# Attention and gated MLP for one token: A_w_down's first chunk in A_wo's column groups, K heads 0 and 1 in two transfers

## The chip, the cores and the metric

The kernel runs on one core of a Trainium2 chip. The core has five engines with instruction streams of their own (TensorE or PE for matmuls, VectorE or DVE, ScalarE or ACT, GpSimd or POOL, SyncE or SP, which here issues the DMAs), an on-chip memory of 128 partitions (SBUF), and a matmul accumulator of 128 partitions by eight banks of 512 float32 (PSUM). The metric is device time in microseconds (us) of one execution, as the median over runs; smaller is better.

## The reference, cut to what matters

One token x of 512 values is normalized, and two branches start from the result. Branch A is attention: 32 query heads over the last 4096 positions of a cache with 8 key and value heads of 128, then the output weight wo. Branch B is a gated MLP of width 1792; with one token in the batch its routing always picks that token, and only the sigmoid of the routing score is left of it.

```python
xn = layernorm(x)
# A: x @ wq -> 32 heads of 128; W = 4096 positions; 4 query heads share one K/V head
scores = einsum("bhqd,bhkd->bhqk", q, k) * 128 ** -0.5
o = softmax(scores) @ v
a = o.reshape(1, 1, 4096) @ wo                      # 4096 x 512
# B: one token, so the top-1 choice is that token
y = (silu(xn @ w_gate) * (xn @ w_up)) @ w_down      # 512 x 1792, 1792 x 512
b = xn + y * sigmoid(xn @ w_r)
return x + a + b
```

All inputs are bfloat16. 30.7 MB are read from device memory: 4.2 MB of wq, 8.4 MB each of K and V, 3.7 MB of w_gate and w_up together, 4.2 MB of wo, 1.8 MB of w_down.

## The kernel before, in words

The program is written out by hand for each engine. `Eng.mark` makes an instruction count up its engine's semaphore, and `Eng.need` makes an engine wait until a semaphore has reached a mark. Each DMA has a semaphore of its own, which sixteen DMA engines count up. `hoist` at the end moves the first issues ahead of the program's start; it changes no order within an engine.

**Transfers.** SP issues all large ones, in this order: wq in two halves (L110, L209), K in four transfers of two heads (L220, `pair`), V in four (L325), then, once the query projection has read wq, w_gate and w_up into wq's place (L327, L328), and, once six K heads have been copied out of `k_sb`, wo in two halves and w_down in four chunks of 7, 4, 2 and 1 rows per partition (L407 to L413) into K's place. They form one queue. A row here is what one partition holds of w_down for one of 14 steps; a chunk of seven rows is 128 pieces of 7 KB.

`pair` brings positions of two heads at once: 64 partitions belong to each head, and a partition's 64 positions of 128 values are 16 KB in one piece. With `steps([0, 2, 4, 6, 8])` each transfer carries two of the kernel's "heads", which are halves of those 64 positions.

**Queries.** TensorE waits for a half of wq and multiplies it with xn in 16 matmuls (L300), four at a time in four column groups of the array (`tile_position`). ACT copies the result (L306), TensorE transposes it in two halves (L320), and DVE spreads each half into `qpad` (`q_out`, L308 to L313). The first half's `q_out` runs right there (L323), the second's stands behind DVE's first two K copies (L354 to L356).

**K stage** (L354 to L405). For each of eight heads DVE copies the head from `k_sb` to `kin` in two halves (`C`, L344), TensorE transposes it in four blocks (`T`, L380), DVE and ACT evacuate the blocks (`E`, L349 and L352), and TensorE multiplies them with the queries (`Sm`, L389) into the two score banks 4 and 5. Then come the softmax (L422 to L445), the V stage with a loop over eight heads (L449 to L504), the gate and up matmuls (L524), and the products behind them on DVE (L535 to L540), which leave w_down's left operand in `hTr`.

**End.** TensorE multiplies wo's 32 rows in four column groups into bank 5 (`grouped`, `a_ps`, L546): row j goes to partition 32 * (j % 4), so that four matmuls of 512 columns run at once, and the first four start the accumulation. DVE adds the four partial rows to the residual (`rf`, zero but for partition 0) and writes `part` (L565). w_down's 14 rows go by halves into banks 0 and 1 (`by_halves`, L551): two column groups, each with 256 columns. Behind the first chunk TensorE adds `part` up over its four partitions with a vector of ones at those places (`sel4`, float32, by halves into the same two banks, L573). Behind the last chunk DVE and ACT each copy one half of the result, and SP sends it out (L578 to L581).

**Fillers.** Matmuls of zeros into bank 7, which nobody reads, stand at many places (`warm`, `fill`; L191): among them two behind the normalization (L268), one before the second half of wq (L295), a loop of five times two before the K stage (L357), four behind L529 (`fill(F4)`), a loop of eight times two between wo's halves (L560), and four behind wo (L564).

Of the kernel before, what the change touches and what calls it, by code (L numbers as in the profile page):

```python
# [9 lines left out]
ALU = mybir.AluOpType  # L10
# [28 lines left out]
def kernel(  # L39
# [15 lines left out]
    P = 128  # L55
    D = A_x.shape[2]
    KT = D // P
    HKV = A_k_cache.shape[1]
# [7 lines left out]
    FB = F // P  # L66
    RJ = (HQ * DH) // P
# [35 lines left out]
    def early(eng, name, out_, in_):  # L103
# [13 lines left out]
    k_sb = sb("k_sb", [P, HKV, 4, 1024], BF16)  # L117
# [7 lines left out]
    qpad = sb("qpad", [P, HKV, 2, 32], BF16)  # L125
# [4 lines left out]
    hTr = sb("hTr", [P, FB, 32], BF16)  # L130
# [5 lines left out]
    zst = sb("zst", [P, P], BF16)  # L136
    zmov = sb("zmov", [P, 512], BF16)
# [18 lines left out]
    oT2 = sb("oT2", [P, RJ], BF16)  # L156
# [7 lines left out]
    ps = nc.alloc_psum_tensor("ps", [P, 8, 512], F32)  # L164
# [3 lines left out]
    qT_ps = ps[:, 6, 0:256].bitcast(BF16).rearrange("p (h c) -> p h c", c=P)  # L168
    pT_ps = ps[:, 0:2, :].bitcast(BF16)
    pv_ps = ps[:, 2, :]  # L170
    a_ps = ps[:, 5, :]
    HD = D // 2
    g_ps = [ps[32 * c:32 * c + 1, c, 0:HD] for c in range(2)]
    rf = kT[:, 0, :].bitcast(F32)
    part = kT[:, 1, :].bitcast(F32)
# [5 lines left out]
    wd_sb = k_flat[:, 0:FB * D]  # L181
    wo_sb = k_flat[:, FB * D:(FB + RJ) * D]

    S = lambda n: nc.alloc_semaphore(n)
    PE, ACT, DVE, POOL, SP = (Eng(nc, nc.tensor, "pe"), Eng(nc, nc.scalar, "act"), Eng(nc, nc.vector, "dve"),
                              Eng(nc, nc.gpsimd, "pool"), Eng(nc, nc.sync, "sp"))
    te, ac, ve, gp, sy = nc.tensor, nc.scalar, nc.vector, nc.gpsimd, nc.sync

    def warm(n):
        for _ in range(n):  # L190
            te.matmul(ps[:, 7, :], lhsT=zst[:], rhs=zmov[:], start=True, stop=True)  # L191

    def fill(n):
        warm(2 * n)

    def ends(ins):
        ends_at[ins.ins.engine] = ins.ins.name
# [14 lines left out]
    def pair(name, tile_, cache, i0, i1):  # L212
        g, n = i0 // 2, (i1 - i0) * NT
        src = cache[0, 2 * g:2 * g + 2, Sk - W:, :].rearrange("h (q t) d -> q h t d", t=TP)
        dst = bass.AP(tile_, i0 * NT * DH, [[HKV * NT * DH, P], [1, n * DH]])
        t0 = (i0 % 2) * NT
        return [dma(sy, f"{name}{i0}", dst, src[:, :, t0:t0 + n, :].rearrange("q h t d -> q h (t d)"))] * (i1 - i0)

    steps = lambda cuts: zip(cuts[:-1], cuts[1:])
    t_k = sum([pair("k", k_sb, A_k_cache, a, b) for a, b in steps([0, 2, 4, 6, 8])], [])  # L220

    c0 = POOL.mark(gp.memset(ident_bf[:], 0.0))
    POOL.need(c0)
# [4 lines left out]
    t_qpad0 = POOL.mark(gp.memset(qpad[:], 0.0))  # L228
# [11 lines left out]
    a = DVE.mark(ve.bn_stats(out=stats[:], in_=xrow[:]))  # L240
# [6 lines left out]
    a = DVE.mark(ve.reciprocal(out=sml[:, 1:2], in_=sml[:, 0:1]))  # L247
# [5 lines left out]
    for kt in range(KT):  # L253
        ins = te.matmul(ps[:, 6, 256 + kt:257 + kt], lhsT=xn_row[:].rearrange("a (p k) -> a k p", k=KT)[:, kt, :],  # L254
                        rhs=ident_bf[0:1, 0:1], start=True, stop=True)
# [9 lines left out]
    t_identf = DVE.mark(ve.tensor_copy(out=ident_f[:], in_=ident_bf[:]))  # L265
    DVE.need(t_rth)
    t_gf = DVE.mark(ve.tensor_scalar(out=sml[:, 4:5], in0=sml[:, 3:4], scalar1=0.25, scalar2=0.25, op0=ALU.mult, op1=ALU.add))
    warm(2)  # L268
    PE.need(t_gf, t_ones)
    t_gfp = PE.mark(te.matmul(ps[:, 6, 264:265], lhsT=ones_f[0:1, :], rhs=sml[:, 4:5], start=True, stop=True))  # L270
    with nc.allow_low_precision(reason="0/1 values are exact in bf16"):
# [4 lines left out]
                                     in_=ident_bf[:].rearrange("p (q h) -> p h q", h=2)))  # L276
# [13 lines left out]
    t_qpad = []  # L290
    for kh in range(2):
        if kh == 1:
            for ch in range(2):
                te.matmul(sc[:, ch, :], lhsT=zst[:], rhs=zmov[:], start=True, stop=False, skip_group_check=True)
            warm(1)  # L295
        PE.need(t_wq[kh], t_ps0)
        for hf in range(2):
            for kt in range(kh * KH, (kh + 1) * KH):
                for c in range(4):
                    ins = te.matmul(ps[32 * c:32 * c + 1, hf, :], lhsT=xnT[:, kt:kt + 1],  # L300
                                    rhs=wq_sb[:, kt, (4 * hf + c) * 512:(4 * hf + c + 1) * 512],
                                    start=(kt == 0), stop=(kt == KT - 1), tile_position=(0, 32 * c))
            if kh == 1:
                t_qp = PE.mark(ins)
                ACT.need(t_qp)
                t_qe.append(ACT.mark(ac.copy(out=q4[:, hf, :], in_=ps[:, hf, :])))  # L306

    def q_out(hf, t_qt):  # L308
        DVE.need(t_qt, t_qpad0)
        for u in range(2):  # L310
            dst = bass.AP(qpad, 2 * hf * 132 + 80 * u, [[HKV * 64, P], [132, 2], [32, 2], [1, 4]])
            t_q = DVE.mark(ve.tensor_copy(out=dst, in_=qT_ps.rearrange("p h (g e r) -> p g e h r", e=2, r=32)[:, :, :, :, 0]))
        t_qpad.append(t_q)  # L313

    for hf in range(2):
        PE.need(t_qe[hf], t_gfb)
        if hf == 1:
            PE.need(t_qpad[0])
        for hl in range(4):
            ins = te.transpose(qT_ps[:, hl, :], q4[:, hf, hl * DH:(hl + 1) * DH], ident_bf[:])  # L320
        t_qt = PE.mark(ins)
        if hf == 0:
            q_out(hf, t_qt)  # L323

    t_v = sum([pair("v", v_sb, A_v_cache, a, b) for a, b in steps([0, 2, 4, 6, 8])], [])  # L325
    SP.need(t_qp)
# [26 lines left out]

    for h in range(2):  # L354
        C(0, h)
    q_out(1, t_qt)  # L356
    with te.Fori(0, 5):  # L357
        warm(2)
    for g in range(HKV):
        pool_q(g)  # L360
        last = (g == HKV - 1)
# [35 lines left out]
    with te.Fori(1, 9) as i:  # L397
# [20 lines left out]
    a = POOL.mark(gp.memset(rf, 0.0))  # L418
    POOL.need(a)
    t_rf = POOL.mark(gp.tensor_copy(out=rf[0:1, :], in_=resid[:]))  # L420
# [13 lines left out]
                              start=True, stop=True))  # L434
# [49 lines left out]
    with te.Fori(1, 9) as i:  # L484
        g = i - 1
# [52 lines left out]
                                           in1=ps[:, 3, 0:FC].rearrange("p (i b) -> p b i", b=FB), op0=ALU.mult, op1=ALU.mult))  # L538
    DVE.need(t_h)
    t_hT = DVE.mark(ve.transpose(out=hTr[:].rearrange("p b i -> p (b i)"), in_=h4[:].rearrange("p b i -> p (b i)")))  # L540
    fill(F4)
    PE.need(t_oT2)

    def grouped(j, lhsT, w):
        c = j % 4
        return te.matmul(a_ps[32 * c:32 * c + 1, :], lhsT=lhsT, rhs=w[:, j * D:(j + 1) * D], start=(j < 4), stop=False,  # L546
                         tile_position=(0, 32 * c), skip_group_check=True)

    def by_halves(lhsT, row, start=False, stop=False):
        for c in range(2):  # L550
            ins = te.matmul(g_ps[c], lhsT=lhsT, rhs=row[:, c * HD:(c + 1) * HD], start=start, stop=stop,  # L551
                            tile_position=(0, 32 * c), skip_group_check=True)
        return ins

    for k, (j0, j1) in enumerate(wo_chunks):
        PE.need(t_wo[k])
        for j in range(j0, j1):
            ins = grouped(j, oT2[:, j:j + 1], wo_sb)
        if k == 0:
            with te.Fori(0, 8):  # L560
                fill(1)
    t_g4 = PE.mark(ins)
    DVE.need(t_g4, t_rf)
    fill(2)  # L564
    t_part = DVE.mark(ve.tensor_tensor(out=part, in0=a_ps, in1=rf, op=ALU.add))  # L565
    PE.need(t_hT)
    for k, (j0, j1) in enumerate(wd_chunks):
        PE.need(t_wd[k])
        for j in range(j0, j1):
            ins = by_halves(hTr[:, j, 0:1], wd_sb[:, j * D:(j + 1) * D], start=(j == 0), stop=(j == FB - 1))  # L570
        if k == 0:
            PE.need(t_part, t_sel4)
            by_halves(sel4[:], part)  # L573
    t_a = PE.mark(ins)
# [38 lines left out]
```

## Time and profile before

| what | value |
|---|---|
| median of 4 runs | 78.96 us (78.89 to 79.05) |
| the profiled execution | 78.89 us |
| its span, first to last instruction | 77.3 us |
| read from device memory | 30.67 MB, mean 397 GB/s over the span |
| busy share: TensorE, its weight loads | 75%, 38% |
| busy share: DVE, ACT, POOL | 57%, 39%, 14% |
| the chain that ended last, by engine | DMA 70%, PE 14%, ACT 6%, DVE 3% |

The busy shares are means over stages with different limits. The chain of waits goes back from the last instruction to what released it, step by step, and so names what the end hangs on. In the rows of the time line the first number is the start in us from the span's start, the second the length, and the bracket names how long the engine idled before and what ended that wait. A row can hold several matmuls of one line (x14), which overlap each other. The granted clock is the one that the throttle granted to TensorE; it is 1.0 throughout. The trace also has one record for each DMA packet (start, length, bytes, queue); sixteen engines work in parallel, each through its own share of every transfer, with a 4-byte packet, the semaphore, behind each share.

### The profile page before, as it was taken

What the parts mean: (1) busy time and instruction counts of PE and PEld (TensorE: products, weight loads), DVE (VectorE), ACT (ScalarE), POOL (GpSimd) and SP (SyncE); (2) the same over time, 40 slices, a digit from 0 to 9 for tenths busy, and PEclk for the clock granted to TensorE, in tenths of its full rate; (3) what the DMA queues carried; (4) which work ended last, traced back from release to release, by engine and by line L of the source; (5) the groups of instructions that cost most, each with busy time, mean ns of one, the idle gap of its engine ahead of it and who ended that gap; (6) DMA issues with size and microseconds to landing.
All of it is one profiled execution on the core that took longest, in us unless ns stands there. A gap on an engine that the chain in (4) does not pass through costs nothing.

```text
span 77.3 us, 1662 instructions
## 1 busy us (share of the span) xinstructions
PE 57.8 (75%) x645; PEld 29.7 (38%) x652; DVE 43.8 (57%) x96; ACT 30.4 (39%) x41; POOL 10.6 (14%) x22
## 2 busy tenths in 40 slices
PE   0015985767989997997995766788887795798891
PEld 0010411426766775685682225222222251343240
DVE  2765900119866956966963762988989248400302
ACT  2771003102895895896775043333343420000001
POOL 3960000000230220220217600000000000000000
DMA  6999999999999999999999999999999999999910
GB/s 136 398 416 407 415 475 432 432 415 407 432 475 441 415 407 415 449 432 441 419 398 424 449 441 432 424 405 423 445 408 465 423 415 407 441 404 405 377 43 1
DMA packets 2601, 30.72 MB, mean 397 GB/s; under 512 B 291, under 2 KB 422, under 8 KB 806
## 3 DMA queue, kind: packets, MB, share of 16 engines
q1 hardware_dynamic: 2594, 30.67, 94.3%
q8 instruction: 2, 0.03, 0.2%
q14 instruction: 1, 0.01, 0.0%
q10 hardware_dynamic: 4, 0.00, 0.0%
HBM read 30.67 MB, written 0.00 MB: 397 GB/s over the span
## 4 chain that ended last, share of the span: by engine, by line
DMA 70%; PE 14%; ACT 6%; DVE 3%; issue 2%; SPq 1%
DMA k_sb<-in_B_w_down_dram 51%; DMA k_sb<-in_A_k_cache_dram 20%; PE ps L380 8%; ACT kT L352 6%; PE ps L551 3%; PE ps L389 3%; DVE kin L344 2%; SPq L202 1%; DVE kT L349 1%; DVE kT L578 1%; SPq L84 0%; SPq L101 0%
## 5 line engine op out<-in xcount | busy, mean ns | idle before, releaser
L352 ACT COPY kT<-ps 128x1024 bf16<-128x1024 bf16 x19 | 18.6, 1016 | 9.5 <-PE ps L380 9.4
L380 PE MATMUL ps<-perm_bf,kin 128*128 128x128 bf16 x256 | 17.1, 220 | 1.4 <-DVE kin L344 1.0
L380 PEld LDWEIGHTS ps<-perm_bf,kin 128*128 128x128 bf16 x256 | 14.3, 98 | 5.8 <-issue 4.3
L344 DVE COPY kin<-k_sb 128x2048 bf16<-128x2048 bf16 x16 | 10.9, 686 | 5.2 <-DMA k_sb<-in_A_k_cache_dram 3.7
L191 PE MATMUL ps<-zmov,zst 128*128 128x512 bf16 x38 | 10.9, 394 | 1.7 <-PEq L84 1.2
L349 DVE COPY kT<-ps 128x1024 bf16<-128x1024 bf16 x13 | 9.0, 691 | 2.9 <-PE ps L380 2.4
L475 ACT CAST pvS<-ps 128x512 bf16<-128x512 f32 x8 | 4.7, 586 | 10.0 <-PE ps L481 10.0
L337 POOL COPY qAB<-qpad 128x64 bf16<-128x64 bf16 x8 | 4.0, 500 | 31.2 <-PE ps L389 31.2
L389 PE MATMUL ps<-kT,qAB 128*32 128x512 bf16 x68 | 6.8, 389 | 1.9 <-ACT kT L352 1.9
L191 PEld LDWEIGHTS ps<-zmov,zst 128*128 128x128 bf16 x45 | 3.9, 99 | 6.2 <-issue 3.3
L455 DVE COPY vin<-v_sb 128x2048 bf16<-128x2048 bf16 x8 | 5.5, 685 | 1.1 <-PE ps L490 1.0
L461 DVE COPY vin<-v_sb 128x2048 bf16<-128x2048 bf16 x8 | 5.5, 683 | 0.0
L490 PE MATMUL ps<-vin,pTcur 128*32 128x512 bf16 x32 | 3.2, 386 | 2.6 <-ACT pvS L475 2.2
L579 ACT CAST kT<-ps 1x256 bf16<-1x256 f32 x1 | 0.4, 363 | 11.9 <-PE ps L551 11.9
L502 PE MATMUL ps<-zmov,zst 128*128 128x512 bf16 x16 | 4.7, 376 | 0.0
L254 PE MATMUL ps<-ident_bf,xn_row 1*128 1x1 bf16 x4 | 0.3, 166 | 5.1 <-POOL qAB L231 5.1
L565 DVE TENSOR_TENSOR kT<-ps,kT 128x512 f32<-128x512 f32 x1 | 0.7, 691 | 5.5 <-PE ps L546 5.5
L300 PE MATMUL ps<-wq_sb,xnT 128*1 128x512 bf16 x32 | 2.9, 499 | 0.8 <-DMA wq_sb<-in_A_wq_dram 0.8
L496 PE MATMUL ps<-vin,pTcur 128*32 128x512 bf16 x32 | 3.2, 387 | 0.3 <-DVE vin L461 0.2
L490 PEld LDWEIGHTS ps<-vin,pTcur 128*32 128x32 bf16 x32 | 1.1, 92 | 6.0 <-DVE vin L455 5.5
L389 PEld LDWEIGHTS ps<-kT,qAB 128*32 128x32 bf16 x68 | 1.9, 92 | 3.9 <-DVE kT L349 1.1
L306 ACT CAST q<-ps 128x512 bf16<-128x512 f32 x2 | 1.1, 588 | 5.3 <-PE ps L300 5.3
(92 smaller groups left out, 52.3 us busy)
## 6 DMA issues: line engine op xcount, KB each, us to landing
k_sb<-in_A_k_cache_dram SPq DMA_DIRECT2D x4, 2048.0 KB, 21.8
v_sb<-in_A_v_cache_dram SPq DMA_DIRECT2D x4, 2048.0 KB, 38.4
wq_sb<-in_A_wq_dram SPq DMA_DIRECT2D x2, 2048.0 KB, 9.1
k_sb<-in_A_wo_dram SPq DMA_DIRECT2D x2, 2048.0 KB, 35.1
wq_sb<-in_B_w_gate_dram SPq DMA_DIRECT2D x1, 1792.0 KB, 43.6
wq_sb<-in_B_w_up_dram SPq DMA_DIRECT2D x1, 1792.0 KB, 47.5
k_sb<-in_B_w_down_dram SPq DMA_DIRECT2D x1, 896.0 KB, 39.1
k_sb<-in_B_w_down_dram SPq DMA_DIRECT2D x1, 512.0 KB, 39.9
```

Source lines behind the costliest of these rows:

```text
L191: te.matmul(ps[:, 7, :], lhsT=zst[:], rhs=zmov[:], start=True, stop=True)
L337: gp.tensor_copy(out=qAB[:], in_=qpad[:, g]).then_inc(s_q, 1)
L344: ve.tensor_copy(out=kin[:, 2 * h:2 * h + 2, :], in_=k_sb[:, g, 2 * h:2 * h + 2, :]).then_inc(s_c[h], 1)
L349: ve.tensor_copy(out=kT[:, b, :], in_=tp[:, b, :]).then_inc(s_ev[b], 1)
L352: ac.copy(out=kT[:, b, :], in_=tp[:, b, :]).then_inc(s_ev[b], 1)
L380: ins = te.transpose(tp[:, b, k * P:(k + 1) * P], kin[:, b, k * P:(k + 1) * P], perm_bf[:])
L389: ins = te.matmul(sc[32 * cq:32 * cq + 32, e, :], lhsT=qAB[:, e, :], rhs=kT[:, b, :].rearrange("d (k h q) -> d h k q", h=2, q=PH)[:, e], s ...
L455: ve.tensor_copy(out=vin[:, 0].rearrange("p (q k) d -> p q (k d)", q=4), in_=v_in[:, :, 0:4 * DH]).then_inc(s_va, 1)
L461: ve.tensor_copy(out=vin[:, 1].rearrange("p (q k) d -> p q (k d)", q=4), in_=v_in[:, :, 4 * DH:]).then_inc(s_vb, 1)
L475: ac.copy(out=pvS[:].rearrange("p t d -> p (t d)"), in_=pv_ps).then_inc(s_pvs, 1)
L490: ins = te.matmul(pv_ps[32 * tl:32 * tl + 32, :], lhsT=pTcur[:, tl].rearrange("p q e r -> p (q e r)"), rhs=vin[:, 0].rearrange("p (q t) d ...
L502: te.matmul(ps[:, 7, :], lhsT=zst[:], rhs=zmov[:], start=True, stop=True)
```

## The change

Four things differ.

- K's first two heads come in two transfers (256 pieces of 8 KB in place of 128 of 16 KB), each with its own semaphore.
- The second half's `q_out` moves up to the first, ahead of DVE's first K copies, and the fillers at L268, L295 and L357 are gone.
- w_down's first chunk of seven rows goes through `grouped`, into bank 5 on top of wo's partial rows. For that bank 5 and the halves of banks 0 and 1 are zeroed by three matmuls of zeros ahead of `fill(F4)`, and no later matmul starts an accumulation there.
- DVE's addition of the residual waits for that chunk, and the matmuls with `sel4` stand behind the second chunk instead of the first. Behind wo there are two fillers in place of four.

```diff
-    def warm(n):
-        for _ in range(n):
+    def fill(n):
+        for _ in range(2 * n):
             te.matmul(ps[:, 7, :], lhsT=zst[:], rhs=zmov[:], start=True, stop=True)
-
-    def fill(n):
-        warm(2 * n)
...
-    t_k = sum([pair("k", k_sb, A_k_cache, a, b) for a, b in steps([0, 2, 4, 6, 8])], [])
+    t_k = sum([pair("k", k_sb, A_k_cache, a, b) for a, b in steps([0, 1, 2, 4, 6, 8])], [])
...
-    warm(2)
     PE.need(t_gf, t_ones)
...
                 te.matmul(sc[:, ch, :], lhsT=zst[:], rhs=zmov[:], start=True, stop=False, skip_group_check=True)
-            warm(1)
...
-    def q_out(hf, t_qt):
-        DVE.need(t_qt, t_qpad0)
-        for u in range(2):
-            dst = bass.AP(qpad, 2 * hf * 132 + 80 * u, [[HKV * 64, P], [132, 2], [32, 2], [1, 4]])
-            t_q = DVE.mark(ve.tensor_copy(out=dst, in_=qT_ps.rearrange("p h (g e r) -> p g e h r", e=2, r=32)[:, :, :, :, 0]))
-        t_qpad.append(t_q)
...
         t_qt = PE.mark(ins)
-        if hf == 0:
-            q_out(hf, t_qt)
+        DVE.need(t_qt, t_qpad0)
+        for u in range(2):
+            dst = bass.AP(qpad, 2 * hf * 132 + 80 * u, [[HKV * 64, P], [132, 2], [32, 2], [1, 4]])
+            t_q = DVE.mark(ve.tensor_copy(out=dst, in_=qT_ps.rearrange("p h (g e r) -> p g e h r", e=2, r=32)[:, :, :, :, 0]))
+        t_qpad.append(t_q)
...
     for h in range(2):
         C(0, h)
-    q_out(1, t_qt)
-    with te.Fori(0, 5):
-        warm(2)
...
+    te.matmul(a_ps, lhsT=zst[:], rhs=zmov[:], start=True, stop=False, skip_group_check=True)
+    for c in range(2):
+        te.matmul(ps[:, c, 0:HD], lhsT=zst[:], rhs=zmov[:, 0:HD], start=True, stop=False, skip_group_check=True)
     fill(F4)
     PE.need(t_oT2)
 
-    def grouped(j, lhsT, w):
+    def grouped(j, lhsT, w, row):
         c = j % 4
-        return te.matmul(a_ps[32 * c:32 * c + 1, :], lhsT=lhsT, rhs=w[:, j * D:(j + 1) * D], start=(j < 4), stop=False,
+        return te.matmul(a_ps[32 * c:32 * c + 1, :], lhsT=lhsT, rhs=w[:, row * D:(row + 1) * D], start=False, stop=False,
                          tile_position=(0, 32 * c), skip_group_check=True)
 
-    def by_halves(lhsT, row, start=False, stop=False):
+    def by_halves(lhsT, row, stop=False):
         for c in range(2):
-            ins = te.matmul(g_ps[c], lhsT=lhsT, rhs=row[:, c * HD:(c + 1) * HD], start=start, stop=stop,
+            ins = te.matmul(g_ps[c], lhsT=lhsT, rhs=row[:, c * HD:(c + 1) * HD], start=False, stop=stop,
                             tile_position=(0, 32 * c), skip_group_check=True)
         return ins
 
     for k, (j0, j1) in enumerate(wo_chunks):
         PE.need(t_wo[k])
         for j in range(j0, j1):
-            ins = grouped(j, oT2[:, j:j + 1], wo_sb)
+            ins = grouped(j, oT2[:, j:j + 1], wo_sb, j)
         if k == 0:
             with te.Fori(0, 8):
                 fill(1)
-    t_g4 = PE.mark(ins)
-    DVE.need(t_g4, t_rf)
-    fill(2)
-    t_part = DVE.mark(ve.tensor_tensor(out=part, in0=a_ps, in1=rf, op=ALU.add))
+    fill(1)
     PE.need(t_hT)
     for k, (j0, j1) in enumerate(wd_chunks):
         PE.need(t_wd[k])
         for j in range(j0, j1):
-            ins = by_halves(hTr[:, j, 0:1], wd_sb[:, j * D:(j + 1) * D], start=(j == 0), stop=(j == FB - 1))
+            if k == 0:
+                ins = grouped(j + RJ, hTr[:, j, 0:1], wd_sb, j)
+            else:
+                ins = by_halves(hTr[:, j, 0:1], wd_sb[:, j * D:(j + 1) * D], stop=(j == FB - 1))
         if k == 0:
+            t_g4 = PE.mark(ins)
+            DVE.need(t_g4, t_rf)
+            t_part = DVE.mark(ve.tensor_tensor(out=part, in0=a_ps, in1=rf, op=ALU.add))
+        if k == 1:
             PE.need(t_part, t_sel4)
             by_halves(sel4[:], part)
```

## The prediction, made before the changed kernel ran

> **What bounds the kernel now.** I read the chain of waits first, then the time line of the last six microseconds, then the table of windows for the DMA at the end, then the trace's DMA packets one by one.
>
> The end of the chain of waits, in order of time (start, length, what):
>
> ```profile
> 34.02 39.12 DMA k_sb<-in_B_w_down_dram
> 73.14 0.14 issue
> 73.27 1.80 PE ps L551 x26
> 75.07 0.00 issue
> 75.08 0.62 PE ps L551 x6
> 75.70 0.03 issue
> 75.72 0.41 DVE kT L578
> ```
>
> The time line of the end (start, length, engine, line):
>
> ```profile
> 70.98 1.03 PE L546 MATMUL ps<-k_sb,oT 128*1 128x512 bf16 x16 [0.21 <-DMA k_sb<-in_A_wo_dram]
> 71.95 1.04 PE L191 MATMUL ps<-zmov,zst 128*128 128x512 bf16 x4
> 72.07 0.69 DVE L565 TENSOR_TENSOR kT<-ps,kT 128x512 f32<-128x512 f32 x1 [5.51 <-PE ps L546]
> 73.27 0.93 PE L551 MATMUL ps<-k_sb,hTr 128*1 128x256 bf16 x14 [0.29 <-DMA k_sb<-in_B_w_down_dram]
> 74.03 0.60 PE L551 MATMUL ps<-kT,sel 128*1 128x256 f32 x4
> 74.44 0.34 PEld L551 LDWEIGHTS ps<-k_sb,hTr 128*1 128x1 bf16 x8 [0.31 <-DMA k_sb<-in_B_w_down_dram]
> 74.47 1.21 PE L551 MATMUL ps<-k_sb,hTr 128*1 128x256 bf16 x14
> 75.07 0.09 PEld L551 LDWEIGHTS ps<-k_sb,hTr 128*1 128x1 bf16 x4 [0.30 <-DMA k_sb<-in_B_w_down_dram]
> 75.40 0.08 PEld L551 LDWEIGHTS ps<-k_sb,hTr 128*1 128x1 bf16 x2 [0.24 <-DMA k_sb<-in_B_w_down_dram]
> ```
>
> The windows (length, five engines, clock, DMA share, GB/s), and the instruction queues' rows of the page:
>
> ```profile
> 72.50:73.00 0.50, 0.49 (x3) 0.00 (x0) 0.26 (x1) 0.00 (x0) 0.00 (x0) 1.00 1.02 391
> 73.50:74.00 0.50, 0.50 (x14) 0.42 (x10) 0.00 (x0) 0.00 (x0) 0.00 (x0) 1.00 0.17 61
> 74.00:74.50 0.50, 0.50 (x10) 0.17 (x8) 0.00 (x0) 0.00 (x0) 0.00 (x0) 1.00 0.14 53
> ...
> q8 instruction: 2, 0.03, 0.2%
> q14 instruction: 1, 0.01, 0.0%
> ```
>
> The kernel is a DMA stream that is full from 1.0 us on. The four pieces of A_w_down reach TensorE at 73.17, 74.44, 75.07 and 75.40, and TensorE's weight loads wait for a DMA before the last three (0.31, 0.30, 0.24 us); only in front of the second were matmuls still running, the selecting ones, to 74.47. The last piece sets the end: 75.40, then 0.3 us of matmul, 0.41 of copy, 1.2 of the output's DMA: span 77.3, and 1.55 around it make the profiled run's 78.89. The median of the four runs, 78.96, is 0.07 above. So only two things count: when the DMA stream ends, and what TensorE does between 73.17 and 75.70.
>
> The windows show that the stream ends raggedly: after 73.5 the rate is 53 to 61 GB/s, two of sixteen engines. In the packets, fourteen engines write their last semaphore by 73.7, one at 74.52, one at 74.92. The last one stood still for 1.02 us at 29.79, while a 16 KB packet of the instruction queue q8 ran (29.78 to 30.82); the other lost its time at 37.89, beside the 8 KB packet of q14.
>
> **The change, part by part.**
>
> *K heads 0 and 1 in two transfers.* 128 pieces of 16 KB become 256 of 8 KB; one more issue on SP (0.59 to 0.66 us by the four K issues), which moves the V issues (4.29 to 8.37 us) back by that. V lands from 37 us on and SP then idles until 13.2 us: nothing. The stream itself gets slower. In the packets one engine takes 4.865 us for eight pieces of 16 KB with their semaphore (first engine done at 6.58, 11.45, 16.32, 21.18), 4.29 for eight of 14 KB (50.49 to 54.78), 2.17 for eight of 7 KB (68.87 to 71.04). A line through 7 and 16 KB gives 0.3085 us for 8 KB; sixteen of them take 4.94 instead of 4.865: +0.07. Halving 14 KB pieces into 7 KB gives 2 x 2.17 - 4.29 = +0.05. The floor is 0; a gain is excluded, since no row has smaller pieces running faster. I take +0.07, the nearest rows; it shifts all that comes after, the last piece too.
>
> The Trainium skill, "DMA: Bandwidth & Descriptors", Specifications, says that a transfer runs at line rate from 512 B up. By it this part would cost 0 and the sum would be 0.07 less; the rows (26.4 GB/s per engine in 7 KB pieces, 26.9 in 16 KB) do not agree with it to that precision.
>
> Head 0 can start after 1 MB. DVE's first copy began at 17.06 after waiting 2.89; half of the 4.87 us earlier is 14.6. q_out(1), two copies of 0.13, now stands before it on DVE and waits for the second transposes (end 14.69), so the copy starts at 15.0. Queued behind q_out on DVE are these copies, and TensorE's first K transposes wait for them. DVE has one more wait, for head 1's own semaphore, before C(1,0), with the evacuation of head 0's third block queued behind it; head 1 lands at about 17.06 and DVE would be there at 17.1: nothing. Head 2 still comes with its transfer: DVE waited 0.86 for it at 21.95. The two microseconds are lost there, and the K stage goes on as before.
>
> *Fillers removed.* Two at 6.58, one at 10.88, ten at 14.75 to 16.9, two of four at 71.95, against three zeroing matmuls more behind L529. The latter cost 0.216 + 2 x 0.109 = 0.43 us after 64.99; A_wo's first half reaches TensorE at 66.07, which covers them and leaves 0.65. The two behind A_wo ended at 72.99, before 73.17: TensorE waits for the DMA instead, 0. The early ones can let the clock fall: the first 16 query matmuls took 1.88 us (8.24), the second 16, after fillers, 1.03 (12.19), at a granted clock of 1.00 in both. If the second also run slow: +0.85, transposes twice 0.4 more, K's first copy at 16.3 instead of 15.0, still before 17.06. Slow K transposes (16 in 1.07 now, 1.95 at that ratio) over heads 0 and 1 could at worst put the compute chain 1 to 2 us late; behind it lie 0.65 before A_wo, 0.2 before its second half, 0.7 before 73.17, together 1.5. I take 0.
>
> The skill's "TensorE: Matmul & The Clock Gate", Part 1, says that an idle window of about 3.4 us halves the clock. That speaks against removing the ten; no run here shows how long an idle stretch the clock bears. With head 0 here at 14.6 TensorE would idle about 1 us in front of the K stage, so by the rule the sum has 0 for these ten as well.
>
> *The tail, where the path is.* In place of 14 half-row matmuls, A_w_down's first seven rows run in four column groups: two rounds. A_wo's 16 give (1.03 - 0.378)/3 = 0.217 a round. From 73.27: 0.217 + 0.378, end 73.87; DVE starts 0.06 later (72.01 to 72.07 now), 0.69: the sum is ready at 74.62. It was ready at 72.76. TensorE meanwhile waits for the second piece anyway (74.44). Then four rows in halves, at (0.93 - 0.272)/6 = 0.109 a row: 74.47 to 74.90. Only now the selecting matmuls, two pairs at 0.217 (0.60 - 0.379): 74.90 to 75.34. The sum is 0.28 early for them. The third piece, here since 75.07, starts at 75.34, two rows to 75.55. The last, here since 75.40, starts at 75.55 instead of 75.40: **+0.15**. Behind it stand the two output copies, SP's wait and the output's DMA, all later by as much.
>
> Put otherwise: between second and last piece TensorE now has 0.436 + 0.434 + 0.218 = 1.09 us of work and 0.96 of time; before it had 0.65. The 0.33 us that the groups save lie in front of the second piece, where TensorE then idles. Bounds: 0 if the pieces come further apart than 1.1 us (no gain, since the last rows can't start before their piece), +0.43 if the selecting matmuls run only behind the last piece.
>
> **Sum.** 78.89 + 0.07 + 0.15 = 79.11 on the profiled run; on the median 78.96 + 0.22 = **79.18 us**.
>
> **Rivals.**
>
> *Faster: the last DMA engine loses its stall.* The end hangs on one engine that lost 1.02 us to an instruction packet at 29.79. The new program has another TensorE stream (some 25 instructions fewer) and other K timing. If the packet meets another engine or time, the end falls to the next-late engine: 74.92 to 74.52, so 79.18 - 0.40 = 78.78; without both stalls, 73.7, it is 77.95. It decides from 0.38 us of lag lost. For: the end is nothing but this lag. Against: four runs within 0.16 us, so the packets fall alike each time, and the K stage is back in step from head 2, before 29.79.
>
> *Same: one of the two small terms is not there.* Pieces of 8 KB at full rate, or the last two pieces of A_w_down arriving 0.1 us further apart: 79.03 to 79.11. Against: both come from rows of the same kind of work.
>
> *Much slower: the clock or a worse lag.* If the compute chain comes more than 1.5 us late through slow K matmuls, A_wo's second half and the tail follow, up to 80.2; if both instruction packets meet the same DMA engine, the end is 0.9 later, 80.1. For: ten fillers stood exactly in front of the K stage. Against: head 0's two microseconds of lead.
>
> *The change doesn't do what it says:* the sum would not be hidden. Its slack is 0.28; were the addition later than that, TensorE would wait in front of the selecting matmuls and each 0.1 would cost 0.1.
>
> **How the numbers follow.** Forecast (79.10 to 79.27) 0.55; one term not there 0.15; last engine's lag shorter 0.20, half of it losing one stall (78.78); much slower 0.10. Such runs can tell 0.2%, 0.16 us, from nothing: slower is above 79.12. Of the forecast 0.02 falls below it. Slower 0.53 + 0.10 = 0.63, same 0.17, faster 0.20. The range goes from 78.77 to 79.46: it takes in one stall lost and the tail's upper bound (78.96 + 0.07 + 0.43 = 79.46), and leaves out half of the lag case and the much slower ones.
>
> **What would show it.** Right: A_w_down's first seven matmuls as one burst of about 0.6 us, the addition at 73.9, the selecting matmuls after eight others and ending near 75.6, no DMA wait before the last two pieces, the last matmuls starting 0.13 to 0.17 after their piece arrived; every semaphore from the second K transfer on later by 0.05 to 0.1. Wrong: a wait for the DMA still in front of the last piece; its arrival moved by more than 0.2 us either way; a TensorE still at half pace at 20 us.

## The result: 0.16% slower, and the profile after

| | before | after |
|---|---|---|
| median | 79.03 us (78 runs) | 79.10 us (52 runs) |
| ratio to before, 95% interval | | 1.0016, 1.0009 to 1.0023 |
| the profiled execution, its span | 78.89 us, 77.3 us | 79.01 us, 77.6 us |

The ratio is +0.13 us, with an interval of +0.07 to +0.18; the two medians lie only 0.07 apart, and without four executions at a lower granted clock, which are taken up below, the means lie 0.09 apart. The forecast was +0.22 (79.18): the way was right, but the forecast is 1.7 times the ratio's size. The measured value lies within 0.2% of before, in the case to which the forecast gave 0.17. That 79.10 lies at the edge of the forecast's band (79.10 to 79.27) is luck: before's median is 79.03 over 78 runs and was 78.96 over four. Counted from before, the band begins at +0.14, and +0.13 belongs to the rival in which one of the two small terms is missing (+0.07 to +0.15).

The end of the chain of waits after the change:

```profile
34.87 39.68 DMA k_sb<-in_B_w_down_dram
74.54 0.04 issue
74.59 1.38 PE ps L541 x18
75.97 0.02 issue
75.99 0.41 DVE kT L572
```

Before, the chain hung on A_w_down's first piece (to 73.14), and TensorE's weight loads still waited for a DMA before each of the last three pieces. Now it hangs on the second piece, at 74.54, and from there TensorE runs without a gap to the end. The time line shows the same stretch:

```profile
71.13 1.03 PE L536 MATMUL ps<-k_sb,oT 128*1 128x512 bf16 x16 [0.21 <-DMA k_sb<-in_A_wo_dram]
72.10 0.60 PE L191 MATMUL ps<-zmov,zst 128*128 128x512 bf16 x2
73.43 0.60 PE L536 MATMUL ps<-k_sb,hTr 128*1 128x512 bf16 x7 [0.73 <-DMA k_sb<-in_B_w_down_dram]
74.08 0.69 DVE L564 TENSOR_TENSOR kT<-ps,kT 128x512 f32<-128x512 f32 x1 [7.09 <-PE ps L536]
74.58 0.31 PEld L541 LDWEIGHTS ps<-k_sb,hTr 128*1 128x1 bf16 x8 [1.06 <-DMA k_sb<-in_B_w_down_dram]
74.59 0.60 PE L541 MATMUL ps<-k_sb,hTr 128*1 128x256 bf16 x8 [0.56 <-DMA k_sb<-in_B_w_down_dram]
75.02 0.60 PE L541 MATMUL ps<-kT,sel 128*1 128x256 f32 x4
75.24 0.41 PEld L541 LDWEIGHTS ps<-k_sb,hTr 128*1 128x1 bf16 x6
75.45 0.49 PE L541 MATMUL ps<-k_sb,hTr 128*1 128x256 bf16 x6
```

The seven grouped matmuls take 0.60, the addition follows at 74.08, and the selecting matmuls come behind the second piece's eight. The last six matmuls, third and last piece, are one row with no bracket: nothing was waited for. The last pair starts at 75.45 + 0.49 - 0.27 = 75.67. Its piece had been written by the last DMA engine at 75.06; before, TensorE started 0.48 behind that packet (74.92 to 75.40), so here it could have started at 75.54. The tail costs 0.13 in this execution.

The DMA packets carry the rest. The first of the sixteen engines needed 4.86 us for K's first 2 MB before (11.45 to 16.31) and 4.90 after (11.53 to 16.43): +0.04. The last engine ends at 74.92 before and 75.06 after; of these 0.14 only 0.04 come from the K pieces, 0.09 stand in the first transfer already (6.58 and 6.67), which the change doesn't touch. The windows (length, five engines, clock, DMA share, GB/s) end as raggedly as before:

```profile
73.00:73.50 0.50, 0.07 (x4) 0.10 (x7) 0.00 (x0) 0.00 (x0) 0.00 (x0) 1.00 1.01 365
73.50:74.00 0.50, 0.50 (x7) 0.03 (x6) 0.00 (x0) 0.00 (x0) 0.00 (x0) 1.00 0.25 90
74.00:74.50 0.50, 0.03 (x3) 0.00 (x0) 0.42 (x1) 0.00 (x0) 0.00 (x0) 1.00 0.13 49
```

### The profile page after: what moved, and what is told of

It reads as the page before. It is cut to its first block, busy times and chain, and to the rows that moved or that the text cites. A ratio compares the mean times of both kernels' runs of the same rounds, so it can differ in the third digit from the quotient of the medians.

```text
span 77.6 us, 1620 instructions
## 1 busy us (share of the span) xinstructions
PE 56.8 (73%) x631; PEld 29.7 (38%) x633; DVE 44.0 (57%) x96; ACT 30.4 (39%) x41; POOL 10.3 (13%) x22
## 4 chain that ended last, share of the span: by engine, by line
DMA 65%; PE 17%; ACT 7%; DVE 4%; issue 2%; SPq 2%
DMA k_sb<-in_B_w_down_dram 51%; DMA wq_sb<-in_A_wq_dram 14%; PE ps L367 9%; ACT kT L342 7%; PE ps L376 3%; PE ps L295 2%; PE ps L541 2%; DVE kin L334 2%; SPq L199 2%; PE ps L307 1%; DVE kT L339 1%; DVE qpad L312 1%; DVE kT L572 1%; SPq L84 0%; SPq L101 0%
## 5 line engine op out<-in xcount | busy, mean ns | idle before, releaser
L367 PE MATMUL ps<-perm_bf,kin 128*128 128x128 bf16 x256 | 18.3, 228 | 1.4 <-DVE kin L334 0.9
L367 PEld LDWEIGHTS ps<-perm_bf,kin 128*128 128x128 bf16 x256 | 15.5, 102 | 5.7 <-issue 4.5
L191 PE MATMUL ps<-zmov,zst 128*128 128x512 bf16 x29 | 7.3, 381 | 0.2 <-issue 0.2
L489 PE MATMUL ps<-zmov,zst 128*128 128x512 bf16 x16 | 4.7, 376 | 0.0
L295 PE MATMUL ps<-wq_sb,xnT 128*1 128x512 bf16 x32 | 3.8, 620 | 1.0 <-DMA wq_sb<-in_A_wq_dram 1.0
L191 PEld LDWEIGHTS ps<-zmov,zst 128*128 128x128 bf16 x30 | 2.5, 97 | 3.5 <-issue 1.3
L312 DVE COPY qpad<-ps 128x16 bf16<-128x16 bf16 x4 | 0.5, 170 | 5.7 <-PE ps L307 5.7
```

The lines of the kernel that those rows point to most:

```text
L367: ins = te.transpose(tp[:, b, k * P:(k + 1) * P], kin[:, b, k * P:(k + 1) * P], perm_bf[:])
```

## The experiments

The theory is that of the prediction: a small term in the DMA stream, a larger one in the tail, nothing from the front. Two rivals were put against it: the clock (the missing fillers make TensorE slow, and that is the loss) and the lag (the end follows the one DMA engine that an instruction packet delayed, and nothing else counts).

### The change's parts alone

**K in two transfers**, nothing else:

```diff
-    ... steps([0, 2, 4, 6, 8])], [])
+    ... steps([0, 1, 2, 4, 6, 8])], [])
```

> The kernel before with K's first two heads in two transfers of 8 KB pieces, and nothing else. Theory (two small terms, the stream and the tail): +0.04 to +0.07 us, every semaphore behind the second K transfer later by that, the tail's waits for its last two pieces still there. Rival (clock): 0.00, the fillers are all there. Rival (the last engine's lag): the lag of the last engine behind the fourteenth, 1.23 us at w_up's semaphores before, changes by more than 0.2 us, and the time with it.

Measured: 79.13 us, ratio 1.0031 (1.0005 to 1.0057). The first engine took 4.91 us for the 2 MB. The wide interval has a cause of its own: three of the twelve executions took 79.70 to 79.89 us at a mean granted clock of 0.978; the nine at 1.00 have a mean of 79.07, against 79.02 (standard error 0.04) for before beside them. So the plain cost is about 0.05, near the theory's lower figure but no further from nothing than the noise, and something else comes on top in some executions, which is taken up below.

**The end alone**, K and fillers at the front as before:

```diff
-            ins = grouped(j, oT2[:, j:j + 1], wo_sb)
+            ins = grouped(j, oT2[:, j:j + 1], wo_sb, j)
...
+            if k == 0:
+                ins = grouped(j + RJ, hTr[:, j, 0:1], wd_sb, j)
...
         if k == 0:
+            t_g4 = PE.mark(ins)
...
+        if k == 1:
             PE.need(t_part, t_sel4)
             by_halves(sel4[:], part)
```

> The kernel before with the change's end alone: first chunk of A_w_down in the column groups, the addition behind it, the selecting matmuls behind the second chunk, two fillers less. Theory: +0.12 to +0.15 us, no wait for a DMA before the last piece's matmuls, and the DMA packets as before. Rival (clock): 0.00, since the early fillers are still there. Rival (lag): the time follows the last engine's semaphore and not the tail, so a lag of 1.2 us means 0.00.

Measured: 79.05 us, ratio 1.0005 (0.9994 to 1.0015): +0.04. That misses the expected 0.12 to 0.15; 0.12 lies just inside the interval, and so does 0.00. The expected end without a DMA wait did not come either, at least in the profiled execution:

```profile
74.42 0.31 PEld L554 LDWEIGHTS ps<-k_sb,hTr 128*1 128x1 bf16 x8 [1.07 <-DMA k_sb<-in_B_w_down_dram]
74.86 0.60 PE L554 MATMUL ps<-kT,sel 128*1 128x256 f32 x4
75.27 0.11 PEld L554 LDWEIGHTS ps<-k_sb,hTr 128*1 128x1 bf16 x4 [0.32 <-DMA k_sb<-in_B_w_down_dram]
75.59 0.08 PEld L554 LDWEIGHTS ps<-k_sb,hTr 128*1 128x1 bf16 x2 [0.21 <-DMA k_sb<-in_B_w_down_dram]
```

Here TensorE still waits for the last piece: it came 75.59 - 74.42 = 1.17 behind the second, more than the 1.09 of work between them. That is the prediction's condition for a tail that costs nothing. In this profile alone three DMA engines, not two, are late: the semaphores of the last piece land at 75.07, 75.35 and 75.55, the others by 74.21. At the second piece only two were late (74.11 and 74.38, the others by 73.23), and between the two pieces lies q8's second packet, which starts at 72.98 here and at 73.37 to 74.99 in every other profile. That this packet made the third engine late is argued from the times; it would explain this one execution's interval, not the median's +0.04. The end alone can't settle the tail; the next group says more.

**The front alone**, K in one first transfer:

```diff
-    warm(2)
...
-            warm(1)
...
-        if hf == 0:
-            q_out(hf, t_qt)
+        DVE.need(t_qt, t_qpad0)
+        for u in range(2):
...
-    q_out(1, t_qt)
-    with te.Fori(0, 5):
-        warm(2)
```

> The kernel before with the change's front alone but one K transfer as before: the second q_out moved up, the fillers at three places gone. Theory: 0.00 (within 0.05 us), though the second half of the query matmuls takes 1.9 us instead of 1.0, because head 0 lands at 17 us and the slack of 1.5 us before A_w_down covers what the K stage loses. Rival (clock): this part carries the difference, +0.1 us or more. Rival (lag): the instruction packet of q8 moves away from 29.8 us and the last engine's lag changes by more than 0.2 us, and the time with it.

Measured: 79.03 us, ratio 0.9999 (0.9988 to 1.0010). In the profile TensorE runs at half pace, and the chain of computation is late. First the rows of before, then those of the front alone:

```profile
12.19 1.03 PE L300 MATMUL ps<-wq_sb,xnT 128*1 128x512 bf16 x16 [0.84 <-DMA wq_sb<-in_A_wq_dram]
17.81 1.07 PE L380 MATMUL ps<-perm_bf,kin 128*128 128x128 bf16 x16 [0.95 <-DVE kin L344]
63.93 0.19 PE L529 MATMUL ps<-r,oE 128*128 128x32 bf16 x1
...
12.26 1.88 PE L295 MATMUL ps<-wq_sb,xnT 128*1 128x512 bf16 x16 [1.08 <-DMA wq_sb<-in_A_wq_dram]
17.89 1.89 PE L367 MATMUL ps<-perm_bf,kin 128*128 128x128 bf16 x16 [2.18 <-DVE kin L334]
65.83 0.19 PE L516 MATMUL ps<-r,oE 128*128 128x32 bf16 x1
71.35 1.03 PE L533 MATMUL ps<-k_sb,oT 128*1 128x512 bf16 x16
```

The matmul ahead of the A_wo stage (L529, now L516) is 1.90 late; A_wo's first half starts 0.65 late (66.83), its second 0.37 (71.35), and A_w_down's first piece is met at 73.28, where it was 73.24. So 1.9 us of lateness are absorbed, and the clock rival falls for this part.

The fillers that are gone are not the only thing that sets the early pace. The kernel before, profiled again, took 1.88 us for these 16 query matmuls with all its fillers, and the split alone 1.80; the kernel with the selecting matmuls last, shown below, has none of the early fillers and took 1.03.

**The changed kernel with the end of before:**

```diff
-            if k == 0:
-                ins = grouped(j + RJ, hTr[:, j, 0:1], wd_sb, j)
...
         if k == 0:
-            t_g4 = PE.mark(ins)
...
-        if k == 1:
             PE.need(t_part, t_sel4)
```

> The changed kernel with the end of before: K in two transfers, the front as changed, selecting matmuls behind the first chunk. Theory: the tail term is gone, the stream term stays: +0.04 to +0.07 us on before, so 0.08 to 0.13 faster than the changed kernel. Rival (clock): as slow as the changed kernel, +0.13 or more. Rival (lag): follows the last engine's semaphore only.

Measured: 79.11 us, ratio 1.0037 (1.0010 to 1.0064). Five of twelve executions took 79.57 to 79.90 at a granted clock of 0.978; the seven at 1.00 have a mean of 79.02 (standard error 0.03), as before beside them. On those the theory's 0.04 is neither contradicted nor shown, and 0.07 is unlikely. Over all twelve the expected 0.08 to 0.13 below the changed kernel did not come.

### More and less work behind the second piece

**The selecting matmuls behind the last piece:**

```diff
-        if k == 1:
+        if k == 3:
             PE.need(t_part, t_sel4)
-            by_halves(sel4[:], part)
+            ins = by_halves(sel4[:], part, stop=True)
```

> The changed kernel with the selecting matmuls behind A_w_down's last chunk instead of the second. Theory (TensorE's work behind the pieces is on the path): two pairs of 0.217 us all lie behind the last piece, +0.43 on the end of before, so about +0.3 on the changed kernel. Rival (lag: only the last engine's semaphore counts): no more than the changed kernel.

Measured: 79.43 us, ratio 1.0054 (1.0035 to 1.0074): +0.43 on before, and 0.30 more than the changed kernel, as the theory had it.

```profile
75.53 0.08 PEld L541 LDWEIGHTS ps<-k_sb,hTr 128*1 128x1 bf16 x2 [0.23 <-DMA k_sb<-in_B_w_down_dram]
75.54 0.19 PEld L541 LDWEIGHTS ps<-kT,sel 128*1 128x1 f32 x4
75.64 0.60 PE L541 MATMUL ps<-kT,sel 128*1 128x256 f32 x4
76.29 0.36 ACT L573 CAST kT<-ps 1x256 bf16<-1x256 f32 x1 [13.53 <-PE ps L541]
```

TensorE waits 0.23 for the last piece and then does what it could have done before. With the same K transfers and the same last semaphore as the changed kernel (75.05 and 75.06), only the place of four matmuls differs: the end does not follow the lag alone.

**The tail's work ahead of the second piece:**

```diff
-    wd_chunks = [(0, 7), (7, 11), (11, 13), (13, 14)]
+    wd_chunks = [(0, 5), (5, 11), (11, 13), (13, 14)]
...
-        if k == 1:
+        if k == 0:
             PE.need(t_part, t_sel4)
```

> The changed kernel with A_w_down cut into 5, 6, 2 and 1 rows in place of 7, 4, 2 and 1, and the selecting matmuls behind the first chunk again. Theory: the first piece comes 0.55 us earlier, the sum is ready before the second piece, the selecting matmuls fill that wait, and TensorE waits for each of the last two pieces: 0.07 to 0.12 us faster than the changed kernel, 0.00 to +0.05 on before. Rival (lag): as the changed kernel, within what the last engine's semaphore moves.

Measured: 79.02 us, ratio 0.9999 (0.9988 to 1.0010), where the changed kernel has 1.0016.

```profile
73.36 0.69 DVE L564 TENSOR_TENSOR kT<-ps,kT 128x512 f32<-128x512 f32 x1 [6.51 <-PE ps L536]
74.11 0.60 PE L541 MATMUL ps<-kT,sel 128*1 128x256 f32 x4 [0.78 <-DVE kT L564]
74.54 1.23 PE L541 MATMUL ps<-k_sb,hTr 128*1 128x256 bf16 x18
75.50 0.08 PEld L541 LDWEIGHTS ps<-k_sb,hTr 128*1 128x1 bf16 x2 [0.21 <-DMA k_sb<-in_B_w_down_dram]
```

Five rows arrive sooner, the addition is done by 74.05, the selecting matmuls end where the second piece starts, and the wait for the last piece is back. K's two transfers and the front are as in the changed kernel. So these two together cost 0.00, with an interval of ±0.09, and against the changed kernel's +0.13 the tail is the larger term.

### The same kernels profiled once more

> The kernel before, unchanged, profiled once more. Theory: the two instruction packets are not tied to a place in the program, so q8's first one falls at another time than 29.8 us, the last engine still ends 1.1 to 1.4 us behind the fourteenth, and its last semaphore moves by up to 0.2 us with nothing changed. Rival (lag tied to the program): the packet at 29.8 us again, within 0.1, and the last semaphore within 0.05 of 74.92.

> The changed kernel, unchanged, profiled once more. Theory: the first selecting matmuls start at once behind the second piece's four rows and the tail costs 0 to 0.15 us, by how far apart the second and the last piece come in this execution. Rival (lag tied to the program): q8's first packet at 23.8 us again.

Measured, from the packets (us): start of q8's two packets in the kernel, last semaphore of the fifteenth and of the last engine; then the interval between A_w_down's second and last piece, from the last landing of each one's semaphores.

```
                       q8     q8     15th   last   interval
before                 29.78  74.76  74.52  74.92  0.97
before again           30.38  74.74  74.69  74.92  0.96
end alone              29.75  72.98  74.90  75.12  1.17
front alone            43.26  74.22  74.68  74.96  0.98
changed                23.78  74.99  74.97  75.06  0.96
changed again          47.08  74.33  74.55  75.06  0.91
K split alone          21.46  74.54  74.40  75.21  0.98
changed, end of before 36.57  74.29  74.48  74.98  0.97
select last            45.17  73.60  74.57  75.05  0.95
five rows              23.72  74.25  74.52  75.01  0.97
```

The first packet is not tied to a place in the program: the changed kernel had it at 23.8 and at 47.1, and the last engine ended at 75.06 both times. The kernel before, repeated, had it only 0.6 later (30.38) and ended at the same 74.92, so that pair alone would not tell the theory from its rival. No profile is without the packet, and wherever it falls within the full stream, one engine is about a microsecond late to the end. That takes the ground from the faster rival, which needed the packet's place to matter. The repeated changed kernel (79.16 us) has the tail as in the first profile:

```profile
74.63 0.60 PE L541 MATMUL ps<-k_sb,hTr 128*1 128x256 bf16 x8 [0.59 <-DMA k_sb<-in_B_w_down_dram]
75.06 0.60 PE L541 MATMUL ps<-kT,sel 128*1 128x256 f32 x4
75.50 0.49 PE L541 MATMUL ps<-k_sb,hTr 128*1 128x256 bf16 x6
```

Last pair at 75.72, its packet at 75.06 + 0.48 = 75.54: 0.18, a little over the expected 0 to 0.15. With the first profile, 0.13 to 0.18, round the 0.15 of the prediction.

### Attempts at a faster end

**Quarters of 128 columns, one copy of 128 columns**, on the kernel before, and then in three chunks:

```diff
+    def by_quarters(lhsT, row, start=False, stop=False):
+        for c in range(4):
+            ins = te.matmul(ps[32 * c:32 * c + 1, 0, 0:QD], lhsT=lhsT, rhs=row[:, c * QD:(c + 1) * QD], ...)
...
+    ve.tensor_copy(out=kT[:, 2, 0:QD], in_=ps[:, 0, 0:QD]).then_inc(s_res, 1)
+    t_out = dma(sy, "out", out.rearrange("a b (c n) -> (a b c) n", c=4), bass.AP(kT, 2 * 1024, [[32 * 4096, 4], [1, QD]]))
```

> The kernel before (K in one first transfer, all its early fillers) with another end: the selecting matmuls run ahead of A_w_down's first piece, A_w_down's rows go by quarters of 128 columns into four column groups of one bank, and DVE alone copies the result, 128 columns instead of 256. Theory: behind the last piece a row takes 0.05 us less at best and the copy 0.1 to 0.15 less: -0.10 to -0.20 us on before. Rival (lag): TensorE's program is some 60 instructions longer, an instruction packet falls elsewhere, and the time moves by the last engine's lag, either way.

> As the one before, with A_w_down in three chunks of 8, 4 and 2 rows: no pieces of 1 KB. Theory: the stream's end 0.10 us earlier (eight pieces in 2.47 + 1.28 + 0.66 instead of 2.17 + 1.28 + 0.66 + 0.42 us), one row more behind the last piece, 0.05 to 0.11: within 0.05 us of the one before. Rival (lag): any difference follows the last engine's semaphore.

Measured: 79.29 us, ratio 1.0032 (1.0019 to 1.0045), and 79.26 us, 1.0029 (1.0016 to 1.0042). Both miss the gain. The first one's end:

```profile
75.37 0.09 PEld L553 LDWEIGHTS ps<-k_sb,hTr 128*1 128x1 bf16 x4 [0.22 <-DMA k_sb<-in_B_w_down_dram]
75.66 0.29 DVE L579 CAST kT<-ps 128x128 bf16<-128x128 f32 x1 [2.90 <-PE ps L553]
75.97 0.66 SPq L202 DMA_DIRECT2D out_dram<-kT  x1
```

The copy does save 0.12 (0.41 to 0.29), and the output's DMA is issued 0.19 earlier (76.16 to 75.97). But its last packet lies at 77.30, where it lay at 76.96: from four partitions it takes 1.33 from issue to end instead of 0.80, its issue alone 0.66 instead of 0.32. What the end's arithmetic saves, the output's four pieces take back with interest. The three chunks change nothing beyond 0.05, as expected.

**A shorter TensorE program**, the version with five rows less its later fillers:

```diff
-    W3, F1, F2, F3, F4 = 2, 2, 1, 1, 2
+    W3, F1, F2, F3, F4 = 2, 2, 0, 0, 0
...
-    fill(1)
     PE.need(t_hT)
```

> The version with 5, 6, 2 and 1 rows, with eight filler matmuls less behind the score stage, behind L529 and behind A_wo (F2, F3, F4 and the last fill gone): TensorE's program falls from 528 to 508 instructions. Theory: as that version, within 0.05 us, or the first q8 packet is gone because the program fits two blocks of 16 KB, and then 0.3 to 0.5 us faster, since the end falls to the engine that q14 delays. Rival (clock): the softmax's matmuls run at half pace and the end is later by 0.1 us or more.

> The same with all fillers from the score stage on gone, those of the V loop and between A_wo's halves too: 487 instructions. Theory: as the one before in the packets; TensorE idles more, so slower matmuls in the V stage and at the end, +0.1 to +0.5 us, if the clock falls; 0 if not. Rival (lag): only the last engine's semaphore counts, and the time follows it.

(The second sets all five to 0 and drops the loop between A_wo's halves too.) Measured: 79.08 us, ratio 1.0010 (0.9995 to 1.0024), and 79.11 us, 1.0013 (0.9996 to 1.0031). Neither program loses a q8 packet: first ones at 42.2 and 23.3, last engine at 75.16 and 75.20. The second one's granted clock by slices of 1.9 us:

```profile
PEclk9999999999999999999999955555555555555999
```

Half the clock from the 24th slice to the 37th, some 45 to 72 us, and in eight of the ten executions the time moves by 0.1%: the V stage has that much cover there. The other two took 80.44 and 80.59 at granted clocks of 0.81 and 0.83; neither was profiled. No version here beats the kernel before.

## What stayed open in the first group, and one profile that shows it

Where K comes in two transfers, some executions are longer by 0.3 to 0.9 us, at a mean granted clock of 0.978: three of twelve with the split alone, five of twelve with the changed front and the old end, four of the changed kernel's 54 executions on record (79.31 to 79.74). The kernel before shows that clock twice in 80 executions beside these experiments, at 79.07 and 79.11, without extra time, and the front alone, with K in one transfer, has 0.956 to 0.978 in five of eleven executions, also without (78.89 to 79.06). So it is not the mean that counts but where the slow stretch lies: 0.978 is what 3.41 us at half clock make of a span of 77.6 us, wherever they fall. In the kernel with the selecting matmuls last, the profiled execution happened to be of this kind. Its time line and windows:

```profile
12.28 1.03 PE L295 MATMUL ps<-wq_sb,xnT 128*1 128x512 bf16 x16 [0.74 <-DMA wq_sb<-in_A_wq_dram]
15.75 1.07 PE L367 MATMUL ps<-perm_bf,kin 128*128 128x128 bf16 x16 [0.95 <-DVE kin L334]
62.85 0.19 PE L516 MATMUL ps<-r,oE 128*128 128x32 bf16 x1
66.32 1.65 PE L536 MATMUL ps<-k_sb,oT 128*1 128x512 bf16 x16 [1.97 <-DMA k_sb<-in_A_wo_dram]
```

```profile
64.00:66.00 2.00, 0.35 (x2) 0.00 (x0) 1.46 (x2) 0.00 (x0) 0.00 (x0) 1.00 0.98 418
66.00:68.00 2.00, 1.68 (x17) 0.47 (x18) 0.00 (x0) 0.00 (x0) 0.00 (x0) 0.65 1.00 426
68.00:70.00 2.00, 2.00 (x5) 0.63 (x6) 0.00 (x0) 0.00 (x0) 0.00 (x0) 0.50 0.95 401
```

In this execution TensorE was fast from the query matmuls on (1.03), so K's first head started at 15.75 instead of 17.81, and the chain of computation reached L516 at 62.85, 1.1 us before the kernel before and 1.5 before the changed kernel's first profile. TensorE then idled 1.97 us in front of A_wo, and the clock fell to half from about 66.6 to 70. The filler loop between A_wo's halves, 3.63 us long at full clock with 0.2 to spare, took so long that A_wo's second half started at 72.49 instead of 71.13. With the selecting matmuls last that costs nothing (79.41 in this execution, 79.27 to 79.69 in the other five); with the end of before, the lateness of 1.4 runs into four fillers, A_w_down's first 14 matmuls, the addition and the selecting matmuls, all still ahead of the second piece. That this is what the long executions have in common is argued from the granted clock, since none of them was profiled. The split with all early fillers in place has them too; the profile of it began with a slow TensorE (1.80 for the query matmuls), so whether a fast start gives it the same lead is open.

## Why the prediction was right, step by step

**What bounds the kernel.** Right: the order of the end and two engines behind the others came again in every profile, with a third one in the end alone.

**The DMA stream, +0.07.** Mis-sized: 0.04 to 0.05 by the packets (4.86 to 4.90 and 4.91). The times, of executions at full clock, have 0.05 for the split alone and 0.00 for the changed kernel with the end of before; the five rows have 0.00. Each is within its noise of 0.04. The line through 7 KB and 16 KB pieces overstated what halving costs; the row that halves 14 KB pieces, which gave 0.05, was the nearer one and had been set aside. The Trainium skill's "DMA: Bandwidth & Descriptors", Specifications, with line rate from 512 B up, is off by these 0.04 for 8 KB, which the times can't tell from nothing.

**K's lead lost at head 2.** Half wrong. With a slow TensorE the chain ended 0.4 later than before (64.35 to 63.93), with a fast one 1.1 earlier: part of head 0's lead survives.

**Fillers, 0.** Right in the sum: the front alone measured 0.9999. The slack was set at 1.5 us; 1.90 were absorbed, 1.25 of them ahead of A_wo, where the front alone has no zeroing matmuls and so the whole 1.19 us of idle time of before. What the prediction did not see: the pace of the early matmuls differs between two executions of one program (1.03 and 1.88 in the kernel before), so one profile's 1.03 is no sign of what the fillers do; and the lead can cost, since the earlier chain waits longer for A_wo and the clock fell there in the one profile that shows it, after 1.97 us of idling, well short of the window that the prediction quotes.

**The tail, +0.15.** Right in its mechanism and its place, in both profiles of the changed kernel (0.13 and 0.18), and by the experiments that move the same matmuls (+0.43 behind the last piece, foretold as +0.43; 0.00 ahead of the second). Its sum is 0.02 too large by its own rows: it starts the second piece's matmuls at 74.47, where the selecting ones still ran before; without them they can start at 74.44, and 1.09 us of work in 0.96 leaves 0.13. That interval is 0.91 to 0.98 in nine of the ten profiles above, and 1.17 only where a third engine was late; how often that happens was not measured. On the times no run isolates the term: the five rows put it at 0.13, the end alone at 0.04 with an interval from nothing to 0.12.

**Sum.** +0.22 foretold, +0.13 measured, and 0.04 + 0.13 = 0.17 in the changed kernel's own profile, inside the interval. The two corrected terms make 0.17 to 0.18, so 0.04 to 0.05 of the 0.09 too much are found; the rest is within the noise, and no run says which term it belongs to.

**Rivals.** Faster by a lost stall: it fell, the stall comes whenever the packet comes. The same, one of the two small terms not there: its band is the one that came true; the tail is seen in the traces, so if a term is missing it is the stream's, which the packets show as 0.04 and the times can't tell from nothing. Much slower by the clock: not as foretold (late computation), though a fallen clock goes with 0.2 to 0.6 us more in four of 54 executions. That the sum would not be hidden: it was, ready at 74.77 with the selecting matmuls at 75.02.

## What to carry to other kernels

Where a stream's last pieces arrive a fraction of a microsecond apart, add up the work that each engine has between the arrivals, not its total: with the same four matmuls ahead of the second piece the kernel cost nothing more than before, behind it 0.13 us and behind the last 0.43. A difference of two nearly equal durations out of one profile is a weak number; profile the same kernel twice before leaning on it. A stage that ends earlier in front of a fixed arrival need not be free either: in one profile here the idling was followed by half the clock in the work behind it.

## What the runs showed of the hardware

One 16 KB packet of the instruction queue q8 came in the middle of every one of these programs, at 21 to 47 us, and at 23.8 and 47.1 in two executions of the same program, and a second one at 73 to 75; the DMA engine that the first met stood still for 1.0 us (29.79 to 30.81 in the kernel before) and stayed that much behind to the end. The Trainium skill's "Runtime: NRT & Kernel Launch", Instruction fetch mechanics, has instructions fetched in blocks of 16 KB, 256 instructions, which is the packet's size. Programs of 508 and 487 TensorE instructions, by the count that stands in the expectations above, so less than two such blocks, had the packet just the same.

The output's 1 KB from one partition took 0.80 us from its issue to its last packet, the same 1 KB from four partitions 1.33.

The granted clock's record moves in steps of 3.41 us (half from 66.60 to 70.02 in the kernel with the selecting matmuls last; the other stretches inside the kernels are multiples of it). In the step ahead of that fall TensorE idled 1.97 us, in one stretch. Ahead of the falls of the two shorter programs, at 47.9 and 44.3, it idled 1.93 and 2.17 by the matmuls' records, in stretches of at most 1.33. A step with 1.60 us of idling (11.99 to 15.40, selecting matmuls last) was followed by no fall, one with 1.55 (to 75.98, quarters) by one, so no sharp limit is shown. The record's first entry stands at 11 to 23 us, or, as in the kernel before, there is none; the 1.00 that the views show without one is no measurement: the 16 query matmuls at 8.64 us in the changed kernel took 1.88, where the same number at 12.19 in the kernel before took 1.03.
